# A SwiGLU feed-forward kernel: the first 512 rows of x transposed by the DMA crossbar instead of TensorE

## Chip, cores and metric

The kernel runs on one core of one Trainium2 chip. The metric is device time in microseconds (us) of one execution. A run counts as slow only when it is over 1.5% above the fastest of its kernel.

Words used below. *fc* is one block of 128 columns of the hidden dimension (12 of them). *Piece* is 128 rows (or more) of x that one DMA brings. *fc 0* is the first projection, gate and up. *Crossbar* is short here for a DMA that transposes on its way (`dma_start_transpose`). *Warm-ups* are matmuls on constants that do no work for the result; they are there to bring up TensorE's clock. `pg` and `pu` are the sums of gate and up. "The weights of fc 1 and 2" are two loads of 320 KB, one of `w_gate` and one of `w_up`. SyncE and ScalarE each have a queue on which they issue DMAs. Landing times are read from the trace's completion records of each DMA, in us from the start of the span.

## The reference

```python
B, S, D, F = 1, 2048, 640, 1536          # all tensors bf16
def reference(x, w_gate, w_up, w_down):
    g = silu(x @ w_gate)
    u = x @ w_up
    return (g * u) @ w_down
```

The projections contract over D, so x is needed transposed, with D on the partitions.

## The kernel before

x is taken in four blocks of 512 rows. For blocks 1 to 3 a transposing DMA writes `xT` long before it is needed. Block 0 is needed at once; there x is loaded plainly and transposed by TensorE.

```python
    load_x(nc.sync, 0, 2)                      # 256 rows, plain
    load_w(nc.scalar, wg_sb, wg_v, 0, 1)
    for c in range(2, SUB):                    # SUB = 4
        load_x(nc.sync, c, c + 1)              # 128 rows each
    load_w(nc.sync, wu_sb, wu_v, 0, 1)
    for a, b in W_CHUNKS[1:]:                  # (1,3), (3,6), (6,9), (9,12)
        load_w(nc.sync, wg_sb, wg_v, a, b)
        load_w(nc.sync, wu_sb, wu_v, a, b)
    nc.sync.dma_start(out=wd_sb[:], in_=wd_v)
    for sb in range(1, NSB):
        nc.sync.dma_start_transpose(out=xT[:, :, s_sl], in_=xt_v[s_sl])   # s_sl: 512 rows
    # ... cut ...
    warm(N_WARM)                               # 8 matmuls on constants

    def transpose_chunk(c):
        pt = psum.tile([P, KD, P], bf16, tag="gu", name="pt", bufs=4)
        for kd in range(KD):                   # KD = 5
            nc.tensor.transpose(out=pt[:, kd, :],
                in_=x_sb[:, c, kd * P : (kd + 1) * P], identity=ident[:])
        nc.vector.tensor_copy(out=xT[:, :, c * P : (c + 1) * P], in_=pt[:])
    # ... cut ...
    for c in range(SUB - 1):
        transpose_chunk(c)
    # block 0, fc 0 (all other fc: one proj of 512 columns each for pg and pu)
                proj(pg, wg_sb, fc, sb, 0, h1)         # h1 = 256
                proj(pg, wg_sb, fc, sb, h1, h2)        # h2 = 384
                transpose_chunk(SUB - 1)
                proj(pu, wu_sb, fc, sb, 0, h2)
                proj(pg, wg_sb, fc, sb, h2, S_BLK)
                proj(pu, wu_sb, fc, sb, h2, S_BLK)
    # ... then Silu, product, and the down projection of the block ...
```

Of the kernel before, what the change touches and what calls it, by code (L numbers as in the profile page):

```python
# [7 lines left out]


@with_exitstack  # L10
def kernel(
    ctx: ExitStack,
    tc: tile.TileContext,
    x: bass.AP,
    w_gate: bass.AP,
    w_up: bass.AP,
    w_down: bass.AP,
    out: bass.AP,
):
    nc = tc.nc  # L20
    P = nc.NUM_PARTITIONS
    f32 = mybir.dt.float32
    bf16 = mybir.dt.bfloat16
    ACT = mybir.ActivationFunctionType
    ALU = mybir.AluOpType

    B, S0, D = x.shape
    F = w_gate.shape[1]
    S = B * S0
    x2 = x.rearrange("b s d -> (b s) d")  # L30
    out2 = out.rearrange("b s d -> (b s) d")

    KD = D // P
    KF = F // P
    S_BLK = 512
    NSB = S // S_BLK
    SUB = S_BLK // P
    DA = 512
    N_WARM = 8
    W_CHUNKS = [(0, 1), (1, 3), (3, 6), (6, 9), (9, 12)]  # L40
    assert D % P == 0 and F % P == 0 and S % S_BLK == 0 and D > DA and SUB >= 2

    consts = ctx.enter_context(tc.tile_pool(name="consts", bufs=1))
    work = ctx.enter_context(tc.tile_pool(name="work", bufs=3))
    outp = ctx.enter_context(tc.tile_pool(name="outp", bufs=3))
    psum = ctx.enter_context(
        tc.tile_pool(name="psum", bufs=2, space=bass.MemoryType.PSUM)
    )

    ident = consts.tile([P, P], bf16)  # L50
    x_sb = consts.tile([P, SUB, D], bf16)
    xT = consts.tile([P, KD, S], bf16)
    wg_sb = consts.tile([P, KD, F], bf16)
    wu_sb = consts.tile([P, KD, F], bf16)
    wd_sb = consts.tile([P, KF, D], bf16)
    aT = consts.tile([P, KF, S], bf16)

    make_identity(nc, ident[:])

    x_v = x2.rearrange("(c p) d -> p c d", p=P)  # L60
    xt_v = x2.rearrange("s (kd p) -> s kd p", p=P)
    wg_v = w_gate.rearrange("(kd p) f -> p kd f", p=P)
    wu_v = w_up.rearrange("(kd p) f -> p kd f", p=P)
    wd_v = w_down.rearrange("(kf p) d -> p kf d", p=P)

    def wslice(a, b):
        return slice(a * P, b * P)

    def load_w(eng, dst, src, a, b):
        eng.dma_start(out=dst[:, :, wslice(a, b)], in_=src[:, :, wslice(a, b)])  # L70

    def load_x(eng, c0, c1):
        eng.dma_start(out=x_sb[:, c0:c1, :], in_=x_v[:, c0:c1, :])

    load_x(nc.sync, 0, 2)
    load_w(nc.scalar, wg_sb, wg_v, 0, 1)
    for c in range(2, SUB):
        load_x(nc.sync, c, c + 1)
    load_w(nc.sync, wu_sb, wu_v, 0, 1)
    for a, b in W_CHUNKS[1:]:  # L80
        load_w(nc.sync, wg_sb, wg_v, a, b)
        load_w(nc.sync, wu_sb, wu_v, a, b)
    nc.sync.dma_start(out=wd_sb[:], in_=wd_v)
    for sb in range(1, NSB):
        s_sl = slice(sb * S_BLK, (sb + 1) * S_BLK)
        nc.sync.dma_start_transpose(out=xT[:, :, s_sl], in_=xt_v[s_sl])

    try:
        ones = nc.const_aps.tensor(1.0, [P, S_BLK], bf16)
    except Exception:  # L90
        ones_t = consts.tile([P, S_BLK], bf16)
        nc.vector.memset(ones_t[:], 1.0)
        ones = ones_t[:]

    def warm(n):
        pw = psum.tile([P, S_BLK], f32, tag="gu", name="pw", bufs=4)
        for _ in range(n):
            nc.tensor.matmul(pw[:], lhsT=ones[:, 0:P], rhs=ones, start=True, stop=True)  # L98

    warm(N_WARM)  # L100

    def transpose_chunk(c):
        pt = psum.tile([P, KD, P], bf16, tag="gu", name="pt", bufs=4)
        for kd in range(KD):
            nc.tensor.transpose(  # L105
                out=pt[:, kd, :], in_=x_sb[:, c, kd * P : (kd + 1) * P], identity=ident[:]
            )
        nc.vector.tensor_copy(out=xT[:, :, c * P : (c + 1) * P], in_=pt[:])  # L108

    def proj(ps, w_sb, fc, sb, c0, c1):  # L110
        for kd in range(KD):
            nc.tensor.matmul(  # L112
                ps[:, c0:c1],
                lhsT=w_sb[:, kd, fc * P : (fc + 1) * P],
                rhs=xT[:, kd, sb * S_BLK + c0 : sb * S_BLK + c1],
                start=(kd == 0),
                stop=(kd == KD - 1),
            )

    for c in range(SUB - 1):  # L120
        transpose_chunk(c)

    for sb in range(NSB):
        s_sl = slice(sb * S_BLK, (sb + 1) * S_BLK)
        for fc in range(KF):
            pg = psum.tile([P, S_BLK], f32, tag="gu", name="pg", bufs=4)
            pu = psum.tile([P, S_BLK], f32, tag="gu", name="pu", bufs=4)
            if sb == 0 and fc == 0:
                h1, h2 = (SUB - 2) * P, (SUB - 1) * P
                proj(pg, wg_sb, fc, sb, 0, h1)  # L130
                proj(pg, wg_sb, fc, sb, h1, h2)
                transpose_chunk(SUB - 1)
                proj(pu, wu_sb, fc, sb, 0, h2)
                proj(pg, wg_sb, fc, sb, h2, S_BLK)
                proj(pu, wu_sb, fc, sb, h2, S_BLK)
            else:
                proj(pg, wg_sb, fc, sb, 0, S_BLK)
                proj(pu, wu_sb, fc, sb, 0, S_BLK)
            sg = work.tile([P, S_BLK], f32)
            nc.scalar.activation(sg[:], pg[:], ACT.Silu)  # L140
            nc.vector.tensor_tensor(  # L141
                out=aT[:, fc, s_sl], in0=sg[:], in1=pu[:], op=ALU.mult
            )

        for j in range(SUB):
            s0 = sb * S_BLK + j * P
            last = sb == NSB - 1 and j == SUB - 1
            po_a = psum.tile([P, DA], f32, tag="po_a", name="po_a")
            for kf in range(KF):
                nc.tensor.matmul(  # L150
                    po_a[:],
                    lhsT=aT[:, kf, s0 : s0 + P],
                    rhs=wd_sb[:, kf, 0:DA],
                    start=(kf == 0),
                    stop=(kf == KF - 1),
                )
            po_b = psum.tile([P, D - DA], f32, tag="po_b", name="po_b")
            for kf in range(KF):
                nc.tensor.matmul(  # L159
                    po_b[:],  # L160
                    lhsT=aT[:, kf, s0 : s0 + P],
                    rhs=wd_sb[:, kf, DA:D],
                    start=(kf == 0),
                    stop=(kf == KF - 1),
                )
            ot = outp.tile([P, D], bf16)
            nc.scalar.copy(ot[:, 0:DA], po_a[:])  # L167
            if not last:
                nc.scalar.copy(ot[:, DA:D], po_b[:])  # L169
                nc.sync.dma_start(out=out2[s0 : s0 + P, :], in_=ot[:])  # L170
            else:
                nc.sync.dma_start(out=out2[s0 : s0 + P, 0:DA], in_=ot[:, 0:DA])
                nc.scalar.copy(ot[:, DA:D], po_b[:])  # L173
                nc.scalar.dma_start(out=out2[s0 : s0 + P, DA:D], in_=ot[:, DA:D])


# [28 lines left out]
```

## Time and profile before

| | before |
|---|---|
| time, median | 166.5 us at prediction, 166.7 to 167.0 beside the later runs |
| span of the profiled run | 165.2 us |
| TensorE busy | 97% |
| first matmul of fc 1 | 8.46 us |
| x complete in SBUF (plain loads) | 5.45 us |
| weights of fc 1 and 2 landed | 7.70 (gate), 8.80 (up) us |

Of the page of the kernel before, the first lines:

```profile
span 165.2 us, 2137 instructions
PE 160.5 (97%) x890; PEld 80.3 (49%) x907; DVE 34.9 (21%) x52; ACT 43.5 (26%) x81; POOL 0.7 (0%) x6
```

TensorE (PE) is the limit. (PEld are its weight loads; DVE is VectorE, ACT ScalarE, POOL GpSimd and, below, SPq the queue of SyncE.) So a change of the first microseconds can pay only by letting the dense stretch start sooner. The chain of waits of the kernel before, its first part (start us, duration us, what; x10 means ten instructions):

```profile
0.77 3.57 PE pw L98 x8
4.34 1.08 PE pt L105 x10
...
5.45 0.50 DVE xT L108
...
5.99 0.99 PE pg L112 x10
6.98 0.28 PE pt L105 x5
7.26 0.81 PE pu L112 x5
8.07 0.28 PE pg L112 x5
8.35 0.28 PE pu L112 x5
8.63 0.22 PE pg L112
...
9.71 1.08 PE pu L112 x5
```

Warm-ups (`pw`), transposes (`pt`), the VectorE copy to `xT`, then fc 0. A full projection of 5 matmuls x 512 columns takes 1.08 us, 0.216 us a matmul. The first transposes take 1.08 us for ten of 128 columns, 0.108 us each: half pace, because TensorE's clock is not up yet (its first record in this trace, 1.0, is at 5.92 us; the column PEclk below reads 1.00 before that too). At full pace they are 0.056 us apart.

The windows of the kernel before show what the DMA engines moved while this went on (last three columns: granted TensorE clock, DMA share, GB/s):

```profile
core 0: us, PE busy (x) PEld busy (x) DVE busy (x) ACT busy (x) POOL busy (x), PEclk, DMA share, GB/s
2.00:6.00 4.00, 3.95 (x22) 2.34 (x21) 1.00 (x3) 0.54 (x1) 0.00 (x0) 1.00 0.99 278
6.00:10.00 4.00, 3.95 (x37) 2.79 (x38) 1.65 (x3) 0.85 (x2) 0.00 (x0) 1.00 1.14 311
```

The DMA engines are full from the start. Finally, the only transposing DMAs that this kernel has, from the view of tile `xT` (durations are minimum, median and maximum of the queue time in ns):

```profile
L86 SPq DMA_TRANSPOSE xT<-in_x_dram x3: 3177/3207/11184, 13.1 to 27.5; - x3
DMA to landing us min/median/max: 5.2/6.0/14.1
```

An issue of 512 rows holds the SyncE queue for 3.2 us (the 11.2 us one began behind the last plain load and ended at 24.27 us, just after that load had landed at 24.13).

### The profile page before, as it was taken

What the parts mean: (1) busy time and instruction counts of PE and PEld (TensorE: products, weight loads), DVE (VectorE), ACT (ScalarE), POOL (GpSimd) and SP (SyncE); (2) the same over time, 40 slices, a digit from 0 to 9 for tenths busy, and PEclk for the clock granted to TensorE, in tenths of its full rate; (3) what the DMA queues carried; (4) which work ended last, traced back from release to release, by engine and by line L of the source; (5) the groups of instructions that cost most, each with busy time, mean ns of one, the idle gap of its engine ahead of it and who ended that gap; (6) DMA issues with size and microseconds to landing.
All of it is one profiled execution on the core that took longest, in us unless ns stands there. A gap on an engine that the chain in (4) does not pass through costs nothing.

```text
span 165.2 us, 2137 instructions
## 1 busy us (share of the span) xinstructions
PE 160.5 (97%) x890; PEld 80.3 (49%) x907; DVE 34.9 (21%) x52; ACT 43.5 (26%) x81; POOL 0.7 (0%) x6
## 2 busy tenths in 40 slices
PE   8999999999999999999999999999999999999992
PEld 2844444455644444455554444445654444445551
DVE  0433333300013333310003333330002233331000
ACT  3042222222332222223232222222232222222222
POOL 1000000000000000000000000000000000000000
PEclk9999999999999999999999999999999999999999
DMA  5999999801110000001110000001111000000121
GB/s 147 294 326 327 362 230 223 160 29 55 40 40 0 0 4 0 0 0 42 68 55 0 0 2 0 0 4 40 40 40 40 4 0 0 0 0 0 46 78 40
DMA packets 18906, 11.27 MB, mean 68 GB/s; under 512 B 9681, under 2 KB 18897, under 8 KB 18897
## 3 DMA queue, kind: packets, MB, share of 16 engines
q1 hardware_dynamic: 18096, 10.95, 24.2%
q10 hardware_dynamic: 800, 0.20, 0.5%
q8 instruction: 7, 0.11, 0.3%
q14 instruction: 3, 0.02, 0.0%
HBM read 6.55 MB, written 2.62 MB: 56 GB/s over the span
## 4 chain that ended last, share of the span: by engine, by line
PE 97%; issue 1%; DVE 0%; ACT 0%
PE pg L112 31%; PE pu L112 31%; PE po_a L150 25%; PE po_b L159 7%; PE pw L98 2%; PE pt L105 1%; DVE xT L108 0%; ACT ot L173 0%
## 5 line engine op out<-in xcount | busy, mean ns | idle before, releaser
L112 PE MATMUL pg<-xT,wg_sb 128*128 128x512 bf16 (+2 forms) x244 | 59.5, 371 | 0.4
L112 PE MATMUL pu<-xT,wu_sb 128*128 128x512 bf16 (+2 forms) x241 | 59.6, 375 | 0.2
L141 DVE TENSOR_TENSOR aT<-sg,pu 128x512 bf16<-128x512 f32 x48 | 33.0, 687 | 109.2 <-PE pu L112 108.0
L140 ACT ACTIVATE sg<-pg 128x512 f32<-128x512 f32 x48 | 28.7, 597 | 76.2 <-PE pg L112 76.2
L150 PE MATMUL po_a<-wd_sb,aT 128*128 128x512 bf16 x185 | 43.4, 379 | 0.3
L112 PEld LDWEIGHTS <-wu_sb 128*128 128x128 bf16 x245 | 23.7, 98 | 27.9
L112 PEld LDWEIGHTS <-wg_sb 128*128 128x128 bf16 x250 | 24.0, 98 | 27.2 <-issue 0.2
L150 PEld LDWEIGHTS <-aT 128*128 128x128 bf16 x192 | 18.3, 98 | 19.8
L167 ACT CAST ot<-po_a 128x512 bf16<-128x512 f32 x16 | 9.4, 585 | 40.4 <-PE po_a L150 38.0
L159 PEld LDWEIGHTS <-aT 128*128 128x128 bf16 x192 | 12.1, 98 | 3.8
L159 PE MATMUL po_b<-wd_sb,aT 128*128 128x128 bf16 x192 | 13.3, 220 | 0.1
L98 PE MATMUL pw<-const-bfloat16-1.0 128*128 128x512 bf16 x8 | 3.6, 625 | 0.8 <-PEq L189 0.8
L169 ACT CAST ot<-po_b 128x128 bf16<-128x128 f32 x15 | 4.0, 265 | 1.1
L108 DVE COPY xT<-pt 128x640 bf16<-128x640 bf16 x4 | 2.0, 490 | 5.8 <-PE pt L105 5.7
L105 PEld LDWEIGHTS <-x_sb 128*128 128x128 bf16 x20 | 2.0, 133 | 0.6 <-DMA x_sb<-in_x_dram 0.5
L105 PE MATMUL pt<-ident,x_sb 128*128 128x128 bf16 x20 | 2.2, 289 | 0.0
L98 PEld LDWEIGHTS <-const-bfloat16-1.0 128*128 128x128 bf16 x8 | 1.0, 137 | 2.4 <-issue 2.4
L140 ACT ACT_TABLE_LOAD x1 | 1.3, 1283 | 1.3 <-PEq L189 1.3
masks.py:199 POOL TENSOR_SCALAR_AFFINE_SELECT ident<-ident 128x128 bf16<-128x128 bf16 x1 | 0.3, 292 | 0.1
L173 ACT CAST ot<-po_b 128x128 bf16<-128x128 f32 x1 | 0.3, 265 | 0.0
masks.py:197 POOL MEMSET ident<- 128x128 bf16 x1 | 0.2, 204 | 0.3 <-POOLq L189 0.3
L189 POOL MEMSET const-bfloat16-1.0<- 128x1 bf16 x1 | 0.1, 101 | 0.0
(3 smaller groups left out, 0.3 us busy)
## 6 DMA issues: line engine op xcount, KB each, us to landing
out_dram<-ot SPq DMA_DIRECT2D x15, 160.0 KB, 1.8
wd_sb<-in_w_down_dram SPq DMA_DIRECT2D x1, 1920.0 KB, 12.5
wg_sb<-in_w_gate_dram SPq DMA_DIRECT2D x3, 480.0 KB, 7.0
wu_sb<-in_w_up_dram SPq DMA_DIRECT2D x3, 480.0 KB, 7.6
x_sb<-in_x_dram SPq DMA_DIRECT2D x1, 320.0 KB, 3.2
x_sb<-in_x_dram SPq DMA_DIRECT2D x2, 160.0 KB, 3.7
wg_sb<-in_w_gate_dram SPq DMA_DIRECT2D x1, 320.0 KB, 5.0
wu_sb<-in_w_up_dram SPq DMA_DIRECT2D x1, 320.0 KB, 5.5
```

The costliest lines, as they stand in the source:

```text
L98: nc.tensor.matmul(pw[:], lhsT=ones[:, 0:P], rhs=ones, start=True, stop=True)
L105: nc.tensor.transpose(out=pt[:, kd, :], in_=x_sb[:, c, kd * P : (kd + 1) * P], identity=ident[:])
L108: nc.vector.tensor_copy(out=xT[:, :, c * P : (c + 1) * P], in_=pt[:])
L112: nc.tensor.matmul(ps[:, c0:c1], lhsT=w_sb[:, kd, fc * P : (fc + 1) * P], rhs=xT[:, kd, sb * S_BLK + c0 : sb * S_BLK + c1], start=(kd == 0 ...
L140: nc.scalar.activation(sg[:], pg[:], ACT.Silu)
L141: nc.vector.tensor_tensor(out=aT[:, fc, s_sl], in0=sg[:], in1=pu[:], op=ALU.mult)
L150: nc.tensor.matmul(po_a[:], lhsT=aT[:, kf, s0 : s0 + P], rhs=wd_sb[:, kf, 0:DA], start=(kf == 0), stop=(kf == KF - 1),)
L159: nc.tensor.matmul(po_b[:], lhsT=aT[:, kf, s0 : s0 + P], rhs=wd_sb[:, kf, DA:D], start=(kf == 0), stop=(kf == KF - 1),)
L167: nc.scalar.copy(ot[:, 0:DA], po_a[:])
L169: nc.scalar.copy(ot[:, DA:D], po_b[:])
L173: nc.scalar.copy(ot[:, DA:D], po_b[:])
L189: nc = _bacc.Bacc("TRN2", target_bir_lowering=False, num_devices=1)
```

## The change

The intent: take the 20 transposes and four copies of the first block off TensorE and VectorE, start projecting as soon as the first 128 rows are there, and keep the weights from queueing behind x by issuing them from ScalarE.

```diff
-    N_WARM = 8
+    N_WARM = 6
...
-    load_x(nc.sync, 0, 2)
     load_w(nc.scalar, wg_sb, wg_v, 0, 1)
-    for c in range(2, SUB):
-        load_x(nc.sync, c, c + 1)
-    load_w(nc.sync, wu_sb, wu_v, 0, 1)
-    for a, b in W_CHUNKS[1:]:
+    load_xT(0, P)                              # transposing DMA on SyncE, 128 rows
+    load_w(nc.scalar, wu_sb, wu_v, 0, 1)
+    for c in range(1, SUB):
+        load_xT(c * P, P)
+    load_w(nc.scalar, wg_sb, wg_v, 1, 3)
+    load_w(nc.scalar, wu_sb, wu_v, 1, 3)
+    for a, b in [(3, 6), (6, 9), (9, 12)]:
         load_w(nc.sync, wg_sb, wg_v, a, b)
         load_w(nc.sync, wu_sb, wu_v, a, b)
...
-    for c in range(SUB - 1):
-        transpose_chunk(c)
...
-                proj(pg, wg_sb, fc, sb, 0, h1)
-                proj(pg, wg_sb, fc, sb, h1, h2)
-                transpose_chunk(SUB - 1)
-                proj(pu, wu_sb, fc, sb, 0, h2)
-                proj(pg, wg_sb, fc, sb, h2, S_BLK)
-                proj(pu, wu_sb, fc, sb, h2, S_BLK)
+            for c in range(SUB):
+                proj(pg, wg_sb, fc, s0, c * P, (c + 1) * P)
+                proj(pu, wu_sb, fc, s0, c * P, (c + 1) * P)
```

(Cut: the removal of the identity, `x_sb` and `transpose_chunk`, and a regrouping of the rest into functions that changes no instruction.)

More of the change, by code (lines that the diff above doesn't have):

```diff
@@ L6 @@
 from concourse._compat import with_exitstack
-from concourse.masks import make_identity
 @with_exitstack
@@ L38 @@
     DA = 512
-    N_WARM = 8
-    W_CHUNKS = [(0, 1), (1, 3), (3, 6), (6, 9), (9, 12)]
+    N_WARM = 6
     assert D % P == 0 and F % P == 0 and S % S_BLK == 0 and D > DA and SUB >= 2
@@ L48 @@
     )
-    ident = consts.tile([P, P], bf16)
-    x_sb = consts.tile([P, SUB, D], bf16)
     xT = consts.tile([P, KD, S], bf16)
@@ L56 @@
     aT = consts.tile([P, KF, S], bf16)
-    make_identity(nc, ident[:])
-    x_v = x2.rearrange("(c p) d -> p c d", p=P)
     xt_v = x2.rearrange("s (kd p) -> s kd p", p=P)
@@ L64, with load_xT @@
     wd_v = w_down.rearrange("(kf p) d -> p kf d", p=P)
-    def wslice(a, b):
-        return slice(a * P, b * P)
     def load_w(eng, dst, src, a, b):
-        eng.dma_start(out=dst[:, :, wslice(a, b)], in_=src[:, :, wslice(a, b)])
-    def load_x(eng, c0, c1):
-        eng.dma_start(out=x_sb[:, c0:c1, :], in_=x_v[:, c0:c1, :])
-    load_x(nc.sync, 0, 2)
+        fs = slice(a * P, b * P)
+        eng.dma_start(out=dst[:, :, fs], in_=src[:, :, fs])
+    def load_xT(s0, n):
+        nc.sync.dma_start_transpose(out=xT[:, :, s0 : s0 + n], in_=xt_v[s0 : s0 + n])
     load_w(nc.scalar, wg_sb, wg_v, 0, 1)
-    for c in range(2, SUB):
-        load_x(nc.sync, c, c + 1)
-    load_w(nc.sync, wu_sb, wu_v, 0, 1)
-    for a, b in W_CHUNKS[1:]:
+    load_xT(0, P)
[5 more added lines that the diff above has]
+    for a, b in [(3, 6), (6, 9), (9, 12)]:
         load_w(nc.sync, wg_sb, wg_v, a, b)
@@ L84, with proj @@
     for sb in range(1, NSB):
-        s_sl = slice(sb * S_BLK, (sb + 1) * S_BLK)
-        nc.sync.dma_start_transpose(out=xT[:, :, s_sl], in_=xt_v[s_sl])
-    try:
-        ones = nc.const_aps.tensor(1.0, [P, S_BLK], bf16)
-    except Exception:
-        ones_t = consts.tile([P, S_BLK], bf16)
-        nc.vector.memset(ones_t[:], 1.0)
-        ones = ones_t[:]
-    def warm(n):
-        pw = psum.tile([P, S_BLK], f32, tag="gu", name="pw", bufs=4)
-        for _ in range(n):
-            nc.tensor.matmul(pw[:], lhsT=ones[:, 0:P], rhs=ones, start=True, stop=True)
-    warm(N_WARM)
-    def transpose_chunk(c):
-        pt = psum.tile([P, KD, P], bf16, tag="gu", name="pt", bufs=4)
-        for kd in range(KD):
-            nc.tensor.transpose(
-                out=pt[:, kd, :], in_=x_sb[:, c, kd * P : (kd + 1) * P], identity=ident[:]
-            )
-        nc.vector.tensor_copy(out=xT[:, :, c * P : (c + 1) * P], in_=pt[:])
-    def proj(ps, w_sb, fc, sb, c0, c1):
+        load_xT(sb * S_BLK, S_BLK)
+    ones = nc.const_aps.tensor(1.0, [P, S_BLK], bf16)
+    pw = psum.tile([P, S_BLK], f32, tag="gu", name="pw", bufs=4)
+    for _ in range(N_WARM):
+        nc.tensor.matmul(pw[:], lhsT=ones[:, 0:P], rhs=ones, start=True, stop=True)
+    def proj(ps, w_sb, fc, s0, c0, c1):
         for kd in range(KD):
@@ L114, in proj @@
                 lhsT=w_sb[:, kd, fc * P : (fc + 1) * P],
-                rhs=xT[:, kd, sb * S_BLK + c0 : sb * S_BLK + c1],
+                rhs=xT[:, kd, s0 + c0 : s0 + c1],
                 start=(kd == 0),
@@ L118, in proj, with gate_up @@
             )
-    for c in range(SUB - 1):
-        transpose_chunk(c)
+    def gate_up(sb, fc):
+        s0 = sb * S_BLK
+        pg = psum.tile([P, S_BLK], f32, tag="gu", name="pg", bufs=4)
+        pu = psum.tile([P, S_BLK], f32, tag="gu", name="pu", bufs=4)
+        if sb == 0 and fc == 0:
+            for c in range(SUB):
+                proj(pg, wg_sb, fc, s0, c * P, (c + 1) * P)
+                proj(pu, wu_sb, fc, s0, c * P, (c + 1) * P)
+        else:
+            proj(pg, wg_sb, fc, s0, 0, S_BLK)
+            proj(pu, wu_sb, fc, s0, 0, S_BLK)
+        sg = work.tile([P, S_BLK], f32, name="sg")
+        nc.scalar.activation(sg[:], pg[:], ACT.Silu)
+        nc.vector.tensor_tensor(
+            out=aT[:, fc, s0 : s0 + S_BLK], in0=sg[:], in1=pu[:], op=ALU.mult
+        )
@@ new lines, in down_part, with down @@
+    def down_part(po, s0, d0, d1):
+        for kf in range(KF):
+            nc.tensor.matmul(
+                po[:],
+                lhsT=aT[:, kf, s0 : s0 + P],
+                rhs=wd_sb[:, kf, d0:d1],
+                start=(kf == 0),
+                stop=(kf == KF - 1),
+            )
+    def down(s0, last):
+        po_a = psum.tile([P, DA], f32, tag="po_a", name="po_a")
+        down_part(po_a, s0, 0, DA)
+        po_b = psum.tile([P, D - DA], f32, tag="po_b", name="po_b")
+        down_part(po_b, s0, DA, D)
+        ot = outp.tile([P, D], bf16, name="ot")
+        nc.scalar.copy(ot[:, 0:DA], po_a[:])
+        if not last:
+            nc.scalar.copy(ot[:, DA:D], po_b[:])
+            nc.sync.dma_start(out=out2[s0 : s0 + P, :], in_=ot[:])
+        else:
+            nc.sync.dma_start(out=out2[s0 : s0 + P, 0:DA], in_=ot[:, 0:DA])
+            nc.scalar.copy(ot[:, DA:D], po_b[:])
+            nc.scalar.dma_start(out=out2[s0 : s0 + P, DA:D], in_=ot[:, DA:D])
@@ L123 @@
     for sb in range(NSB):
-        s_sl = slice(sb * S_BLK, (sb + 1) * S_BLK)
         for fc in range(KF):
-            pg = psum.tile([P, S_BLK], f32, tag="gu", name="pg", bufs=4)
-            pu = psum.tile([P, S_BLK], f32, tag="gu", name="pu", bufs=4)
-            if sb == 0 and fc == 0:
-                h1, h2 = (SUB - 2) * P, (SUB - 1) * P
-                proj(pg, wg_sb, fc, sb, 0, h1)
-                proj(pg, wg_sb, fc, sb, h1, h2)
-                transpose_chunk(SUB - 1)
-                proj(pu, wu_sb, fc, sb, 0, h2)
-                proj(pg, wg_sb, fc, sb, h2, S_BLK)
-                proj(pu, wu_sb, fc, sb, h2, S_BLK)
-            else:
-                proj(pg, wg_sb, fc, sb, 0, S_BLK)
-                proj(pu, wu_sb, fc, sb, 0, S_BLK)
-            sg = work.tile([P, S_BLK], f32)
-            nc.scalar.activation(sg[:], pg[:], ACT.Silu)
-            nc.vector.tensor_tensor(
-                out=aT[:, fc, s_sl], in0=sg[:], in1=pu[:], op=ALU.mult
-            )
@@ L145 @@
-        for j in range(SUB):
-            s0 = sb * S_BLK + j * P
-            last = sb == NSB - 1 and j == SUB - 1
-            po_a = psum.tile([P, DA], f32, tag="po_a", name="po_a")
-            for kf in range(KF):
-                nc.tensor.matmul(
-                    po_a[:],
-                    lhsT=aT[:, kf, s0 : s0 + P],
-                    rhs=wd_sb[:, kf, 0:DA],
-                    start=(kf == 0),
-                    stop=(kf == KF - 1),
-                )
-            po_b = psum.tile([P, D - DA], f32, tag="po_b", name="po_b")
-            for kf in range(KF):
-                nc.tensor.matmul(
-                    po_b[:],
-                    lhsT=aT[:, kf, s0 : s0 + P],
-                    rhs=wd_sb[:, kf, DA:D],
-                    start=(kf == 0),
-                    stop=(kf == KF - 1),
-                )
-            ot = outp.tile([P, D], bf16)
-            nc.scalar.copy(ot[:, 0:DA], po_a[:])
-            if not last:
-                nc.scalar.copy(ot[:, DA:D], po_b[:])
-                nc.sync.dma_start(out=out2[s0 : s0 + P, :], in_=ot[:])
-            else:
-                nc.sync.dma_start(out=out2[s0 : s0 + P, 0:DA], in_=ot[:, 0:DA])
-                nc.scalar.copy(ot[:, DA:D], po_b[:])
-                nc.scalar.dma_start(out=out2[s0 : s0 + P, DA:D], in_=ot[:, DA:D])
@@ L178 @@
+            gate_up(sb, fc)
+        for j in range(SUB):
+            down(sb * S_BLK + j * P, sb == NSB - 1 and j == SUB - 1)
 _INS = ['x', 'w_gate', 'w_up', 'w_down']
```

## The prediction

> **What bounds the kernel now.** TensorE. The busy table gives PE 160.5 of the 165.2 us span (97%), and in the chain of waits PE holds 97%. From 8.84 us on the chain shows one projection (5 matmuls of 512 columns) every 1.08 us, 0.216 us each, without a gap, to 162.2 us; the tail after that is about 3 us. Only the head can pay.
>
> **The head, by the chain and the timeline.** 0.77 to 4.34 us: 8 warm-up matmuls, 0.427 us apart. 4.34 to 5.42: ten TensorE transposes, 0.108 us each (cold pace). 5.45 to 5.95: a VectorE copy of transposed x. 5.99 to 8.63: the rest of the first projection with the last transposes in it. The first projection itself is worth 2.2 us at the warm pace.
>
> **Removed:** 20 transposes (15 take 1.8 us cold, 5 take 0.3 us warm) and four 0.49 us VectorE copies, one of them on the chain: about 2 to 2.6 us of chain.
>
> **Added:** four DMA transposes of 128 rows. The trace has only the 512-row ones: 3.18 us of issue on the SP queue, 5.2 us from issue to landing at best, so 2.0 us after the issue's end. A quarter is then an estimated 0.8 us of issue, the pieces landing at about 3.5, 4.3, 5.1 and 5.9 us if nothing else runs. But the DMA engines will be shared. Where the 512-row ones run (24 to 32 us) the windows show the DMA share full at about 225 GB/s, against 320 to 330 GB/s for plain loads. The Trainium skill, "DMA: Bandwidth & Descriptors", section "Latency and other measured facts", gives 261 GB/s; this trace shows less. 0.66 MB of x then costs about 3.0 us of DMA, and the 0.98 MB of early weights, now issued beside x rather than behind it, another 3 us. So piece 1 lands at 3.5 to 4, the last at an estimated 6.5 to 8 us, and fc 0 ends at 7 to 8.6 us.
>
> **Second danger: the warm-up.** The Trainium skill, "TensorE: Matmul & The Clock Gate", Part 1, says full rate comes only after about 3.4 us of sustained activity in a free-running window; this trace agrees roughly (cold until about 5.6 us, after 4.9 us of steady work). With 6 warm-ups PE goes quiet at 3.3 us, then works in bursts of 0.6 to 1.1 us between pieces. Full rate may come 1 to 3 us later, which costs up to 1.5 us of the dense stretch.
>
> **Sum:** -1.2 us from the transposes after DMA sharing, +0.5 us from the clock: -0.7 us. Predicted 165.8 us, 8 in 10 from 164.3 to 167.6. Faster by over 2%: 0.02; within 2%: 0.94; slower by over 2%: 0.04.
>
> **What would show it.** Right: first real matmul near 3.5 to 4 us; PE idle between pieces, released by the transposing DMA; fc 0 finished before 8.6 us; from then on the same 1.08 us rhythm, and the same tail. Clock step: matmul spacing 0.427 us beyond 6 us. DMA step: last piece landing after 6.5 us, DMA share full from 2 to 8 us.
>
> **What would make it wrong.** A DMA transpose with a large fixed cost, pieces served one after another (1.5 us each or more): fc 0 ends after 9.5 us, slower. A warm-up that fails until after 10 us. Or, the other way, no DMA contention and no clock loss: 164.5 us.

## The result, and the profile after

The changed kernel takes 171.6 us (median of 4 runs, 171.48 to 171.82) against 166.74 us (4 runs): ratio 1.029, 95% interval 1.027 to 1.031. It is slower by 4.9 us. Ratios here and below are the mean time of one kernel's fast runs over that of the other's of the same rounds, so not quite the ratio of the medians quoted.

The chain of waits of the changed kernel, its first part:

```profile
0.73 1.29 SPq L65
...
2.08 1.25 SPq L65
...
3.38 6.38 DMA xT<-in_x_dram
...
9.80 0.48 PE pg L88 x3
10.28 1.07 PE pu L88 x10
11.35 0.21 PE pg L88 x2
11.56 0.53 PE pu L88 x5
...
13.16 1.43 PE pg L88 x5
14.59 1.08 PE pu L88 x5
```

Until 9.8 us the chain is not on TensorE at all, but in the queue of the transposing DMAs (`SPq L65`) and in the third of them. Then TensorE works through the rest of fc 0 at half pace: five matmuls of 128 columns in 0.53 us. From 14.59 us on the old rhythm of 1.08 us is back, to the end. The timeline of the changed kernel, TensorE only, names the waits:

```profile
5.07 0.44 PE L88 MATMUL pg<-xT,wg_sb 128*128 128x128 bf16 x5 [1.59 <-DMA xT<-in_x_dram]
7.32 0.69 PE L88 MATMUL pg<-xT,wg_sb 128*128 128x128 bf16 x5 [1.81 <-DMA xT<-in_x_dram]
9.80 0.48 PE L88 MATMUL pg<-xT,wg_sb 128*128 128x128 bf16 x3 [1.79 <-DMA xT<-in_x_dram]
10.07 1.27 PE L88 MATMUL pu<-xT,wu_sb 128*128 128x128 bf16 x10
```

The four pieces land at 5.03, 7.28, 9.76 and 10.29 us. The brackets show how long TensorE idled before each burst and what ended it. The first burst still ran at full pace (0.055 us apart), the later ones at half. The windows:

```profile
2.00:6.00 4.00, 1.92 (x9) 0.72 (x8) 0.00 (x0) 1.28 (x1) 0.00 (x0) 1.00 1.09 224
6.00:10.00 4.00, 0.89 (x8) 0.72 (x8) 0.00 (x0) 0.00 (x0) 0.00 (x0) 0.61 1.29 220
10.00:14.00 4.00, 4.00 (x34) 3.36 (x33) 0.69 (x1) 0.60 (x1) 0.00 (x0) 0.53 1.09 324
```

Two things changed. The DMA engines are just as full (share 1.09 and 1.29), but move 222 GB/s from 2 to 10 us where before they moved 295. And the granted clock is half from about 6.9 to 13.7 us, just where fc 0 runs. The view of tile `xT` gives the cost of a piece in its queue:

```profile
L65 SPq DMA_TRANSPOSE xT<-in_x_dram x7: 1255/1292/11892, 0.7 to 29.6; - x7
```

Four of these seven are the pieces of block 0. They hold the SyncE queue for 1.25 to 1.29 us each, 5.2 us together, where one issue of 512 rows held it for 3.2.

The balance closes: the first matmul of fc 1 starts at 12.95 us instead of 8.46 (4.5 us later), its first projection still runs partly at half pace (1.48 instead of 1.08 us, 0.4 us), and together these make, to within 0.1 us, the 4.8 us by which the spans differ (170.0 and 165.2).

### The profile page after: what moved, and what is told of

Same layout as the page of the kernel before. It is cut to its first block, busy times and chain, and to the rows that moved or that the text cites. A ratio compares the mean times of both kernels' runs of the same rounds, so it can differ in the third digit from the quotient of the medians.

```text
span 170.0 us, 2132 instructions
## 1 busy us (share of the span) xinstructions
PE 161.2 (95%) x900; PEld 80.5 (47%) x900; DVE 33.0 (19%) x48; ACT 43.6 (26%) x81; POOL 0.2 (0%) x4
## 4 chain that ended last, share of the span: by engine, by line
PE 93%; DMA 4%; SPq 1%; ACT 0%; issue 0%
PE pu L88 31%; PE pg L88 31%; PE po_a L116 24%; PE po_b L116 6%; DMA xT<-in_x_dram 4%; SPq L65 1%; ACT ot L136 0%
## 5 line engine op out<-in xcount | busy, mean ns | idle before, releaser
L88 PE MATMUL pg<-xT,wg_sb 128*128 128x512 bf16 (+1 forms) x255 | 61.6, 373 | 5.2 <-DMA xT<-in_x_dram 5.2
L88 PE MATMUL pu<-xT,wu_sb 128*128 128x512 bf16 (+1 forms) x255 | 61.1, 374 | 0.0
L116 PE MATMUL po_a<-wd_sb,aT 128*128 128x512 bf16 x192 | 44.1, 379 | 0.0
L116 PEld LDWEIGHTS <-aT 128*128 128x128 bf16 x384 | 29.8, 98 | 23.6
L88 PEld LDWEIGHTS <-wg_sb 128*128 128x128 bf16 x255 | 25.0, 101 | 33.3 <-issue 5.9
L88 PEld LDWEIGHTS <-wu_sb 128*128 128x128 bf16 x255 | 25.3, 102 | 27.7
L84 PE MATMUL pw<-const-bfloat16-1.0 128*128 128x512 bf16 x6 | 2.7, 626 | 0.8 <-PEq L158 0.8
```

The lines of the kernel that those rows point to most:

```text
L84: nc.tensor.matmul(pw[:], lhsT=ones[:, 0:P], rhs=ones, start=True, stop=True)
L88: nc.tensor.matmul(ps[:, c0:c1], lhsT=w_sb[:, kd, fc * P : (fc + 1) * P], rhs=xT[:, kd, s0 + c0 : s0 + c1], start=(kd == 0), stop=(kd == K ...
L116: nc.tensor.matmul(po[:], lhsT=aT[:, kf, s0 : s0 + P], rhs=wd_sb[:, kf, d0:d1], start=(kf == 0), stop=(kf == KF - 1),)
```

## The experiments

Theories. **A**: the pieces of x share the DMA engines with weights that are not needed yet (those of fc 1 and 2, now on ScalarE's queue). **B**: four transposing DMAs cost queue time of their own; later **B'**: what stands behind them in the queue pays for it. **C**: TensorE goes quiet, loses its clock, and then runs the first work at half pace. **D**: the order of the instructions in fc 0. All outputs were correct. Unless it says otherwise, the base of an edit is the changed kernel.

| run | median us | ratio to before | last of x landed, us | first matmul of fc 1, us |
|---|---|---|---|---|
| the change | 171.60 | 1.029 | 10.29 | 12.95 |
| e1_w13_behind | 168.79 | 1.012 | 7.88 | 10.34 |
| e2_one_piece | 172.61 | 1.034 | 9.46 | 13.72 |
| e3_warm32 | 170.67 | 1.024 | 10.53 | 12.00 |
| e4_alone | 172.31 | 1.033 | 7.90 | 13.70 |
| e5_scalar_issue_only | 167.86 | 1.005 | 6.52 (plain) | 8.29 |
| e6_crossbar_only | 170.32 | 1.020 | 7.64 | 11.09 |
| e7_two_pieces | 166.73 | 0.998 | 7.10 | 8.50 |
| e8_source_order | 171.63 | 1.028 | 10.14 | 11.82 |
| e9_behind_warm12 | 168.55 | 1.010 | 7.56 | about 9.7 |
| e12_two_pieces_warm6 | 168.27 | 1.009 | 6.88 | 9.95 |
| e10_first_chunk_alone | 167.30 | 1.004 | 6.10 (plain) | 8.58 |
| e11_chunk_alone_split | 167.13 | 1.002 | 6.10 (plain) | 8.61 |
| e13_half_weights | 170.27 | 1.020 | 9.25 (slow run) | – |
| e14_more_weights | 172.32 | 1.032 | 10.62 | 13.41 |
| e15_two_pieces_shared | 171.64 | 1.028 | 10.41 | 12.54 |

### Which cost: sharing, pieces, clock (e1 to e4)

**e1_w13_behind**

```diff
-    load_w(nc.scalar, wg_sb, wg_v, 1, 3)
-    load_w(nc.scalar, wu_sb, wu_v, 1, 3)
+    load_w(nc.sync, wg_sb, wg_v, 1, 3)
+    load_w(nc.sync, wu_sb, wu_v, 1, 3)
```

> The changed kernel (171.6 us) with one edit: the weights of fc 1 and 2 (two times 320 KB) go to the SyncE queue behind the four transposing DMAs instead of onto the ScalarE queue beside them. Theory A (the pieces of x share the DMA engines with weights that are not needed yet): pieces 3 and 4 land by about 7 and 8.3 us instead of 9.8 and 10.3, the first projection ends 1.5 to 2 us earlier, time 169.4 to 170.2 us. Theory B (each of the four transposing DMAs costs its own 1.3 us of issue and they are served one after another; the sharing hardly matters): landings within 0.3 us of before, 171.3 to 171.9 us.

Measured 168.79 us, 2.8 us less than the change, a little better than theory A said. The pieces landed at 5.30, 5.72, 6.76 and 7.88 us. Timeline of this run, TensorE:

```profile
5.34 1.23 PE L88 MATMUL pg<-xT,wg_sb 128*128 128x128 bf16 x10 [1.85 <-DMA xT<-in_x_dram]
6.80 0.48 PE L88 MATMUL pg<-xT,wg_sb 128*128 128x128 bf16 x3 [0.24 <-DMA xT<-in_x_dram]
...
10.34 0.82 PE L88 MATMUL pg<-xT,wg_sb 128*128 128x512 bf16 x3 [0.68 <-DMA wg_sb<-in_w_gate_dram]
```

The wait has moved: x is there in time, and now fc 1 waits for its weights, which the SyncE queue issued only at 6.02 us, after the four pieces, and which landed at 10.30.

**e2_one_piece**: `load_xT(0, S_BLK)` instead of four calls; the weights stay on ScalarE.

> The changed kernel with the first 512 rows of x transposed by one DMA instead of four; weights on the ScalarE queue as in the change. Theory B (cost of each transposing DMA): issue falls from 5.2 us in all to about 3.2, x lands complete at 7 to 8 us instead of 10.3, and although no piece comes early the time falls to 169.5 to 170.5 us. Theory A (sharing): the same bytes share the same engines, x lands at 9 to 10 us, 171 to 172 us.

x landed complete at 9.46 us, within the range of theory A, and 172.61 us, 0.6 us above it. TensorE idled for 6 us and then ran at half pace until 15.1 us, which theory A had not counted. With the weights beside it, one large DMA is not the cure; one piece with the weights behind it and more warm-ups was not run.

**e3_warm32**: `N_WARM = 32`.

> The changed kernel with 32 warm-up matmuls instead of 6, so that TensorE stays busy until about 9.7 us, when the third piece lands. Theory C (the quiet TensorE loses its clock, and 3.4 us of work run at half pace): matmuls of 128 columns run 0.056 us apart from 10.3 us on, fc 0 ends near 12 us, time 169.7 to 170.3 us, that is 1.3 to 1.9 less. Against it (only the landing counts): 171.4 to 172 us. Beside the clock the instruction order of the first projection changes here (the scheduler returns to source order), which matters little as all pieces are there when the warm-ups end.

170.67 us, 0.9 us less than the change; theory C had said 1.3 to 1.9. The matmuls of fc 0 are 0.056 us apart as it said. But the last warm-up ran until 9.9 us and the whole of fc 0 came after it, so fc 1 began at 12.00 us instead of 12.95. This 0.95 us and the 0.4 us of the first projection of fc 1, now at full pace, make the 1.4 us between the two profiled runs (171.82 and 170.44; the medians differ by 0.9). It is less than the clock is worth, as bursts that the change had done early were now done late. (The order of instructions changes here too.)

**e4_alone**: all weights of fc 0 to 2 on SyncE behind the pieces; nothing shares.

> The changed kernel with all early weights behind the four transposing DMAs on the SyncE queue: nothing else uses the DMA engines while x comes. A measurement of the pieces by themselves. Theory B: they still come 1.28 us apart, the issue time of one, at about 4.1, 5.4, 6.7 and 8.0 us. Theory A: what lies between these and the landings of the changed kernel (5.0, 7.3, 9.8, 10.3) is the price of sharing, 1 to 3 us. If they land as late as 9 to 10 us even alone, both are wrong and the transposing DMA itself is slow. The time of the whole is no test here (weights come late): 171 to 173 us.

The pieces landed at 3.62, 4.98, 7.04 and 7.90 us, on average 1.4 us apart, near the 1.28 us that each holds the queue, and the DMA share in the windows from 3 to 8 us was only 0.4 to 0.8. The queue times are those of the changed kernel, where weights share:

```profile
L65 SPq DMA_TRANSPOSE xT<-in_x_dram x4: 1255/1274/1292, 0.7 to 4.7; - x4
DMA to landing us min/median/max: 2.9/3.1/3.7
```

So alone, the pieces are held up by their queue, not by the engines. With the weights of fc 0 beside them (e1) the last one still lands at 7.88 us: 320 KB fit into the gaps. With 640 KB more (the change) it lands at 10.29. At the 326 GB/s of plain loads 640 KB are 2.0 us (an estimate from the rate of the kernel before); the delay is 2.4 us.

### Parts of the change alone, and a repair (e5 to e8)

**e5_scalar_issue_only**, on the kernel before:

```diff
-    load_w(nc.sync, wu_sb, wu_v, 0, 1)
-    for a, b in W_CHUNKS[1:]:
+    load_w(nc.scalar, wu_sb, wu_v, 0, 1)
+    load_w(nc.scalar, wg_sb, wg_v, 1, 3)
+    load_w(nc.scalar, wu_sb, wu_v, 1, 3)
+    for a, b in W_CHUNKS[2:]:
```

> The kernel before (166.8 us; x still transposed by TensorE) with one part of the change alone: the up weights of fc 0 and both weights of fc 1 and 2 are issued from ScalarE beside the loads of x. If sharing the DMA engines is harmful by itself (theory A in its general form), the last two chunks of x land near 6 to 6.5 us instead of 4.9 and 5.5, and the time rises to 167.3 to 168.3 us. If sharing hurts only the transposing DMA (small pieces that lose against bigger ones), the time stays within 0.3 us of 166.8.

167.86 us against 166.97 beside it, in the range of the general form of theory A, at a third of the price, but not by its path. The chunks of x landed at 4.16, 5.21 and 6.52 us (before: 3.92, 4.92, 5.45). That delay itself cost nothing here (fc 1 began at 8.29 us, as TensorE was busy with transposes). What cost is one wait in the timeline of this run:

```profile
10.48 1.25 PE L114 MATMUL pu<-xT,wu_sb 128*128 128x512 bf16 x5 [0.94 <-DMA wu_sb<-in_w_up_dram]
```

The up weights of fc 1, last in ScalarE's queue, now shared with the gate weights of fc 3 to 5 that SyncE issued at 2.2 us, and landed at 10.43 us instead of 8.80. So the expected mechanism (late x) was there, but another wait made the time. The bytes did not move slower: 271 and 308 GB/s in the two windows where before they were 278 and 311. They came in a worse order.

**e6_crossbar_only**: the loads on the queues and in the order of the kernel before (only the first gate weights on ScalarE), x by the four pieces.

> The changed kernel with the loads in the order and on the queues of the kernel before (only the first gate weights on ScalarE, all else behind x on SyncE): the crossbar alone. The four transposing DMAs hold the SyncE queue until 6.0 us (1.28 us each), so the up weights of fc 0 are issued only then and land near 9.4 us. Theory B' (the queue time of the four pieces is a cost of its own, which the weights on ScalarE were to avoid): x complete at about 7.9 us, fc 0 ends at 10.5 to 11.5 us, 169.5 to 171 us. If only sharing matters: as good as the experiment with the weights of fc 1 and 2 behind (168.8) or better.

170.32 us, in the range of theory B'. x was complete at 7.64 us, but the up weights of fc 0, issued at 6.02 us, landed at 8.94, and fc 0 ended at half pace at 11.1 us. So both arrangements lose: weights beside the pieces delay x, weights behind them are themselves late.

**e7_two_pieces**

```diff
-    N_WARM = 6
+    N_WARM = 12
-    load_xT(0, P)
+    load_xT(0, 2 * P)
     load_w(nc.scalar, wu_sb, wu_v, 0, 1)
-    for c in range(1, SUB):
-        load_xT(c * P, P)
-    load_w(nc.scalar, wg_sb, wg_v, 1, 3)
-    load_w(nc.scalar, wu_sb, wu_v, 1, 3)
+    load_xT(2 * P, 2 * P)
+    load_w(nc.sync, wg_sb, wg_v, 1, 3)
+    load_w(nc.sync, wu_sb, wu_v, 1, 3)
... and fc 0 in two pieces of 256 columns
```

> The changed kernel with the three costs found so far reduced together: two transposing DMAs of 256 rows instead of four of 128, the weights of fc 1 and 2 behind them on SyncE, and 12 warm-ups instead of 6. From one piece of 512 rows at 3.38 us of issue and four of 128 at 1.28, a piece of 256 rows should cost about 2.0 us of issue, 4.0 us in all instead of 5.2; the weights of fc 1 are then issued near 4.8 us and land near 9 us instead of 10.3. Expected: x complete by about 7 us, fc 0 ends near 8.5, fc 1 waits for its weights until about 9: 167.0 to 167.8 us, between the kernel before and the experiment with four pieces (168.8).

166.73 us against 166.97 for the kernel before beside it (ratio 0.998, interval 0.997 to 1.000): a little better than expected, level with the kernel before, 4.9 us better than the change. The first piece of 256 rows held the queue for 1.32 us, hardly more than one of 128, the second for 2.30 (2.07 in e12, 1.92 in e15 below): two pieces took 3.3 to 3.7 us in all, where one took 3.2 to 3.4 and four took 5.2. So the queue time is not a fixed cost for each DMA plus one for its rows; what sets it is open. The queue is free at 4.45 us, the gate weights of fc 1 land at 8.40, and fc 1 begins at 8.50. Its chain of waits:

```profile
0.73 5.55 DMA xT<-in_x_dram
...
6.32 0.71 PE pg L87 x5
7.03 0.55 PE pu L87 x5
7.57 0.55 PE pg L87 x5
```

The pieces land at 6.28 and 7.10 us, the second before it is needed, and five matmuls of 256 columns take 0.55 us: full pace. So the crossbar is not bad in itself; here it costs what TensorE's transposes cost.

**e8_source_order.** The framework that builds the kernel had ordered fc 0 otherwise than the source: gate for pieces 0, 1 and part of 2 before the first up. An issue-order constraint on the projections of fc 0 restored the source's order.

> The changed kernel with the order of the first projection forced to that of the source (gate then up for each piece; the built kernel runs gate for three pieces before the first up). Theory D (the order costs: at 9.8 us 30 matmuls are still to do instead of 20): 10 matmuls of 0.107 us less after the third piece, 170.3 to 170.9 us. If only the landings and the clock count: 171.3 to 171.9 us.

171.63 us: theory D misses. The 10 matmuls were saved (fc 1 began at 11.82 us, 1.1 us earlier), but in the profiled run the clock came up only at about 15.4 us (by the spacing of the matmuls; this trace has no clock record) instead of 13.7, and fc 1 began at half pace, 0.427 us a matmul. The four runs spread over 1.0 us (171.07 to 172.07), and only the profiled one, 172.04, has a trace. In that run, what was gained in one place was lost to the clock in another; of the other three nothing is known.

### Pieces and clock, crossed (e9, e12)

**e9_behind_warm12** is e1 with 12 warm-ups; **e12_two_pieces_warm6** is e7 with 6.

> The experiment with the weights of fc 1 and 2 behind the four pieces (168.8 us), with 12 warm-ups instead of 6. There the first projection ran mostly at half pace and ended at 9.5 us, but fc 1 then waited until 10.3 us for its weights, which the SyncE queue issues only at 6.0 us, after the four pieces. If that queue time is what is left (theory B'), a better clock gains nothing: fc 0 ends near 8.4 us, the wait for the weights grows by as much, 168.5 to 169.0 us. If the clock is what is left (theory C): 167.6 to 168.2 us.

> The experiment with two pieces of 256 rows (166.7 us), with 6 warm-ups as in the change instead of 12. Theory C: TensorE is quiet from 3.3 to 6.3 us, the first projection runs at half pace (20 matmuls of 256 columns 0.213 us apart, 4.3 us instead of 2.2), and nothing hides it: 168.0 to 169.2 us. If the number of pieces and the place of the weights did it all: 166.6 to 167.1 us.

Both came out as expected, 168.55 and 168.27 us. With e1 and e7 they make a square (weights of fc 1 and 2 behind the pieces in all four; medians, us; the four come from three rounds, in which the kernel before took 166.80 to 166.97):

| | 6 warm-ups | 12 warm-ups |
|---|---|---|
| four pieces | 168.79 | 168.55 |
| two pieces | 168.27 | 166.73 |

Neither step alone gives more than 0.5 us; together they give 2.1. In e9 fc 0 is done by about 8.4 us, at full pace, and fc 1 waits until about 9.7 us for weights issued at 6.02. In e12 the weights are there (8.18 us), but fc 0 runs at half pace until 9.6 us. Its timeline:

```profile
6.05 1.23 PE L87 MATMUL pg<-xT,wg_sb 128*128 128x256 bf16 x5 [2.57 <-DMA xT<-in_x_dram]
7.07 1.27 PE L87 MATMUL pu<-xT,wu_sb 128*128 128x256 bf16 x5
```

Ten matmuls take 2.09 us from the first start to 8.14, where e7 takes 1.09. Each of the two costs hides behind the other.

### Attempts to beat both (e10, e11)

Both go back to TensorE transposes with 6 warm-ups and load the first 128 rows of x by a DMA of their own. e11 also issues the up weights of fc 0 from ScalarE and splits the weights of fc 1 from those of fc 2.

> An attempt to beat both kernels. The kernel before (TensorE transposes) with the first 128 rows of x loaded by a DMA of their own instead of two chunks in one, and 6 warm-ups instead of 8. In the kernel before, x of the first two chunks lands at 3.9 us while the weights of fc 1 are there at 7.7, so up to 0.8 us of the 8.5 us head could go. If the first landing starts the chain: first transposes at 3.4 to 3.6 us, head shorter by 0.3 to 0.5 us, 166.3 to 166.7 us. If the third and fourth chunk or the half-pace clock hold it: 166.8 to 167.3 us.

> The same attempt, with the up weights of fc 0 issued from ScalarE and the weights of fc 1 loaded apart from those of fc 2, so that fc 1 has its own sooner. If weights gate the shortened head: another 0.1 to 0.4 us less than the attempt before it, 166.1 to 166.6 us. If sharing delays the later chunks of x as in the experiment with ScalarE issue alone: 166.8 to 167.5 us.

167.30 and 167.13 us, beside 166.86: both missed their hope and fell on the other side. The first chunk did land early (3.19 us), but with four DMAs instead of three the third chunk landed at 5.58 us instead of 4.92 and the fourth at 6.10 instead of 5.45; TensorE waited for them, and fc 1 began at 8.58. No version here beats the kernel before by more than noise.

### Does the delay by sharing grow with what shares? (e13 to e15)

**e13_half_weights**: only the gate weights of fc 1 and 2 on ScalarE. **e14_more_weights**: the weights of fc 3 to 5 there as well. **e15_two_pieces_shared**: e7 with the weights of fc 1 and 2 back on ScalarE, its only edit.

> A dose for the sharing theory: the changed kernel (171.6 us) with only the gate weights of fc 1 and 2 (320 KB) on ScalarE beside the pieces of x, the up weights behind them on SyncE. With 0 KB beside them the last piece landed at 7.9 us, with 640 KB at 10.3. Sharing: about half way, 8.8 to 9.4 us, time 169.5 to 170.7 us. If what hurts is only that ScalarE's queue is in use at all: 10 us or later; if only what comes last counts: near 7.9.

> The other end of the dose: the changed kernel with the weights of fc 3 to 5 (960 KB) as well on ScalarE beside the pieces, 1600 KB in all. In the changed kernel the last of the 640 KB landed at 9.5 us, so only the last piece had some time for itself. Sharing to the end: last piece 10.8 to 12 us, time 171.9 to 173 us. If the pieces had already had all their delay: 10.3 us, 171.3 to 171.9 us.

> The experiment with two pieces of 256 rows and 12 warm-ups (166.7 us), with the weights of fc 1 and 2 back on ScalarE as in the change. If sharing is the largest single cost whatever the pieces are: the second piece lands at 9 to 10 us instead of 7.1, time 169.3 to 171 us. If four small pieces were what made sharing dear (each of them losing its turn), less than 1 us is lost: 167 to 167.7 us.

e13: three fast runs, 170.00, 170.27 and 170.43 us; x complete at 9.25 us, between 7.88 and 10.29. The profiled run was an outlier of 543 us in which TensorE ran at about a quarter of its pace until 381 us and at little over a third after that; its landings are quoted because the early DMAs wait for nothing of TensorE's, but they are of a slow run. The time of the fast runs lies where sharing put it, 1.5 us above e1 and 1.3 below the change.

e14: 172.32 us, the last piece at 10.62 us, below the expected 10.8 to 12. The edit did not do what it was meant to: ScalarE's queue took the first of the extra weights only at 8.09 us, so few of them shared. The time lay in the expected range, but in the profiled run the clock came up only at 15.39 us (13.74 in the change), so it does not tell of the dose, whose upper end stays open.

e15: 171.64 us, 4.9 us more than e7 for one edit, and more than expected. The second piece landed at 10.41 us instead of 7.10:

```profile
2.13 8.28 DMA xT<-in_x_dram
...
10.46 1.22 PE pg L87 x5
11.68 1.07 PE pu L87 x5
```

Two pieces are delayed just like four (10.41 and 10.29), so small pieces losing their turn is not the cause. And the longer wait takes the clock with it: 12 warm-ups no longer reach (in the profiled run the clock was up at 3.60 us, so they ended at 4.9 us, where those of e7 lasted until 6.05, and it fell again at 7.01), and `pu` takes 1.07 us where e7 took 0.55.

## Why the prediction was wrong

The direction was named as a danger, and the mechanisms that it named were the right ones; one was missing, the sizes of the others were wrong, and they do not add as the prediction added them. It said 165.8 us (164.3 to 167.6); it was 171.6.

- *TensorE bounds the kernel, only the head can pay.* Right. The rhythm after the head is the same in both traces, and the balance closes with the head alone.
- *"A quarter is then an estimated 0.8 us of issue, the pieces landing at about 3.5, 4.3, 5.1 and 5.9 us if nothing else runs."* This step failed. A quarter of the rows is not a quarter of the queue time: 1.28 us, so 5.2 us for four. Alone (e4) they landed at 3.62, 4.98, 7.04 and 7.90 us. The first was right, the last 2.0 us off, and all of that is queue time: the last one landed 1.9 us after the end of its issue, as the 2.0 us of the prediction had it.
- *"The last at an estimated 6.5 to 8 us"* with sharing. Failed mostly by the same 2 us: the upper end allowed 2.1 us for sharing (e1 against the change shows 2.4), but it came on top of 7.9 us, not of 5.9, and gave 10.29. That "piece 1 lands at 3.5 to 4" failed too: beside the weights of fc 0, which landed at 3.41 and 4.77 us, it landed at 5.03.
- *Weights beside x are a cost of the DMA engines alone.* Incomplete. The prediction did not see the other side: weights *behind* the pieces are late as well (e6, e9), because the queue is held until 6.0 us. Four pieces leave no good place for them; two pieces do (e7).
- *"+0.5 us from the clock."* Too small. With two pieces it is 1.5 us (e12 against e7). In the change, it is at least the 0.9 us that 32 warm-ups gave back (e3). Full rate was to come "1 to 3 us later"; in the profiled run of the change it was lost at 6.92 us and came back at 13.74, where the kernel before had it from 5.92. The prediction had put the cost at "up to 1.5 us" and then counted a third, although the late landings that it feared would make exactly that case. At 9.80 us 30 matmuls of fc 0 were left; at full pace (0.056 us each) they would have been done near 11.5 us, an estimate from the spacing in e3, and not at 12.95.
- *"fc 0 ends at 7 to 8.6 us."* So it became 12.95 us, and the "-1.2 us from the transposes after DMA sharing" of the prediction's sum became a loss: with the clock, 4.5 us until fc 1 begins.
- *"Later" things that would make it wrong.* "Pieces served one after another (1.5 us each or more)" was nearly the case (2.3 us apart in the change), and that sentence would have given the right sign.

Shown: sharing with the weights of fc 1 and 2 costs 2.8 us at four pieces (e1, net of the wait for these weights that putting them behind brings) and 4.9 us at two (e15, the clock it takes along included); piece count and clock cost 2.1 us together (the square). Left open: the delay under more than 640 KB of sharing, what sets the queue time of a transposing DMA, and why the engines, though full, move so little in the change. That transposing and plain packets mix is not enough to explain it: from 3 to 9 us the same mix with x as one DMA (e2) moved 279 GB/s, the change 221, at the same DMA share of 1.22.

The pages drawn on. The Trainium skill, "DMA: Bandwidth & Descriptors", section "Rules for kernel authors", says that spreading DMAs over issuing engines does not help bandwidth, as all run on the same 16 engines; this case agrees (e5: 271 and 308 GB/s against 278 and 311) and adds that it can do harm, through the order of landings. The Trainium skill, "TensorE: Matmul & The Clock Gate", Part 1, gives a free-running window of about 3.4 us; in the changed kernel's trace the clock was up from 3.50 to 6.92 us, 3.41 us, then half for 6.83 us, two such windows, which agrees. Where in such a window a kernel begins is not the same in every run: after the same six warm-ups the clock was up at 3.5 us in the profiled runs of the change and of e4, while in those of e1, e6, e8, e12 and e14 the first matmuls on x (at 4.4 to 6.2 us) ran at half pace. So one profile of a kernel tells the clock of that run alone.

## What to carry to other kernels

When the DMA engines are full from the start, moving a load to another queue does not make it free: ask what lands later for it, and cost the path alone, beside others, and behind others. Splitting a transposing DMA in four to start sooner raised its queue time from between 3.2 and 3.4 us to 5.2 (in two, to at most 3.7), and everything behind it in that queue pays. And a wait at the head of a TensorE-bound kernel is paid twice when it also lets the clock drop; repairs must be tried together, since one cost can hide another (0.2 and 0.5 us alone, 2.1 us together).

## What the Trainium skill lacked or had wrong

- "DMA: Bandwidth & Descriptors", "Latency and other measured facts": gives 261 GB/s for transposing DMAs with a non-contiguous middle dimension, and more for contiguous ones. Here the windows of the kernel before from 24 to 32 us, where the transposing DMAs run, show 224 GB/s. By queue time 512 rows (655,360 bytes) per 3.2 us are 205 GB/s, and 128 rows (163,840 bytes) per 1.28 us are 128 GB/s. The section gives a rate but no queue time by size; four DMAs of 128 rows held the queue 5.2 us, one of 512 rows 3.2 to 3.4 us.
- The same page, "Rules for kernel authors": "A transpose next to ordinary DMAs needs nothing". For the results that held in every run; for the time, 640 KB of plain loads beside the pieces delayed the last of them from 7.88 to 10.29 us, and the mix moved 222 GB/s where plain loads moved 295 (with x as one DMA, in e2, 266).
- "TensorE: Matmul & The Clock Gate", "Why this matters for your kernels": warns of idle gaps over about 3 us. In the changed kernel the clock fell at 6.92 us, in the second of two gaps of 1.59 and 1.81 us with a burst of 0.44 us between them; no gap had reached 3 us. In e15 it fell at 7.01 us after one gap of 1.98 us.
- The same page, Part 1, mentions a clock seen stuck at a quarter for 50 us and more. One run of e13 stayed near a quarter until 381 us of its 541.5 (matmuls of 512 columns mostly 0.840 us apart instead of 0.216; after that mostly 0.621), and the trace held no clock record for it, so its mean granted clock still read 1.0. The same column reads 1.00 in the first microseconds of every run, where matmuls are plainly at half pace (0.427 us apart): read the spacing, not the column, before the first change of clock.
